# Fused attention and feed-forward on one core: a new load order, a weight product by halves, six banks for value blocks, and zeros in the opening's gaps

## The chip, the cores and the metric

The kernel runs on one core of a Trainium2 chip. The metric is the device time of one execution in microseconds. The comparison uses the median of repeated runs; the profile is of one execution. TensorE multiplies matrices into PSUM (eight banks), ScalarE (ACT) and VectorE (DVE) copy and transform, GpSimd (POOL) and SyncE (SP) here mostly issue DMAs.

## The reference

Inputs are float32: q, k, v of shape (8, 12, 448, 64), two gains of 64, and four weights.

```python
q_n, k_n = rmsnorm(q, g_q), rmsnorm(k, g_k)          # over head_dim = 64
attn = softmax(q_n @ k_n.T / sqrt(64))               # per batch and head, 448 x 448
x = (attn @ v), heads side by side                   # (3584, 768)
a, b = x @ w1, x @ w2                                # (3584, 1024)
out = ((a * b) @ w3) @ w_out                         # (3584, 768)
```

## The kernel before

**Work units.** Attention is cut into 24 units of four heads: three units make one batch of 448 tokens. The norms of q and k are taken on ACT and DVE, q and k are transposed (units 0 to 4 on TensorE, the later ones by DMA), and a unit then has seven score blocks (`do_score`, L626). Each score block is exponentiated by ACT straight out of two PSUM banks (L648). When all seven are done, a value block follows: `do_pv_main` (L711) multiplies the exponentials with ones (for the sums) and with the even and the odd value columns, three kinds in all. Two units are mostly taken together (`start_pv` with size 2); their last 64 rows then go as row-packed matmuls in `do_pv_rest` (L690). A value block of size 2 starts when `PV_BANKS` banks are free, and for as many kinds as there are free pairs of banks the row-packed part goes first; for the others it comes at the end. While a value block is ready and waits for banks, no score and no new pair is started.

**Feed-forward.** w3 and w_out are multiplied with each other first: w3 arrives in eight pieces (`load_w3`), each is transposed on TensorE (`do_w3_turn`, L1071) and copied, and then a "pair" (`w34_pair`) makes 128 rows of the product w3 w_out. A pair holds two PSUM banks and consists of passes of four 64x64 matmuls (L799 in `do_pass`); in the second half of a pair the two row halves swap banks. Between the halves stands `hand_over`: a no-operation on SP (on POOL, once w2 is in) that waits for the first half's last matmul and that the second half waits for. The passes of each half that need the second half of w_out wait for it. Afterwards `ffn1_pair` multiplies x with w1 and w2, and `ffn2_pair` multiplies a*b with the product; those are pairs too. The third buffer for exponentials lies in w_outs, so it comes free when the product is complete.

**Order.** A planner in the kernel lays all instructions out in program order, with costs and due times of its own. TensorE's next step is chosen in `pe_try`: value blocks, transposes, the running pair, scores, a new pair. At most `MAX_PAIRS` pairs are open. A score goes ahead of a running pair only when it is `hungry`, that is when ACT is nearly out of work. The loads that convert weights and v to bfloat16, and q and k of units 1 to 5, are issued by POOL in the order of `POOL_ORDER`:

```python
    POOL_ORDER = (
        "w0 w1 o0 w2 o1 q1 v0 w3 w4 q2 w5 v1 w6 w7 v2 a0 a1 a2 q3 b0 v3 b1 q4 b2 q5".split()
    )
```

Here w is a piece of w3, o a half of w_out, a and b are thirds of w1 and w2, q stands for q and k of a unit, and v for the four loads of a unit's values. A load is issued by POOL only when the one eight before it has landed.

**Start and end.** TensorE starts on matmuls of zeros (`warm`, L1226). The last 128 rows of the output are made by `do_last` (L991) in two parts, each stored by two DMAs (L1005); the other tiles are stored by two DMAs of 64 partitions each from SP (L938).

Of the kernel before, what the change touches and what calls it, by code (L numbers as in the profile page):

```python
# [195 lines left out]
def kernel(  # L196
# [43 lines left out]

    N_PE_T = 5
    QUAD = 13.0
    WARM = 18
    MAX_PAIRS = 2
    MARGIN = 0.25
    LOW = 2
    PV_BANKS = 4
    SOON = 0
    AHEAD_W3 = 4
    EARLY = 4  # L250
    STOCK = 14
    PACE = 1.7
    POOL_ORDER = (
        "w0 w1 o0 w2 o1 q1 v0 w3 w4 q2 w5 v1 w6 w7 v2 a0 a1 a2 q3 b0 v3 b1 q4 b2 q5".split()
    )
    ON_POOL = (1, 2, 3, 4, 5)

# [510 lines left out]
    running = [None]  # L768

    class Pair:  # L770
        def __init__(self, name, nk, n, ready, sides, evacuate):
            self.name, self.nk, self.n = name, nk, n
            self.sides, self.evacuate = sides, evacuate
            self.phase, self.pos, self.gap_at = 0, 0, 0.0
            self.needs = ready

        def ready(self):
            return max(self.gap_at, self.needs(self.pos))

    def hand_over(p, mm, t):  # L780

        at = t + 0.23
        e = "SP" if max(w_at["w2"]) == INF else "POOL"
        nop = (nc.sync if e == "SP" else nc.gpsimd).nop()  # L784
        tc.add_manual_dep(
            nop.ins, mm.ins.name, SYNC_DEP, reason="first half of the sums complete"
        )
        free[e] = max(free[e], at)
        p.gap_at = free[e] + 0.15
        p.nop = nop  # L790

    def do_pass(p, t):
        took = pass_us(p.n) + into("n")
        first = None
        for r in range(2):
            z = r ^ p.phase
            lhsT, rhs = p.sides[z](p.pos)
            for h in range(2):
                mm = nc.tensor.matmul(  # L799
                    out=ps_all[64 * h : 64 * h + 64, p.bank + z, 0 : p.n],  # L800
                    lhsT=lhsT[64 * r : 64 * r + 64, 64 * h : 64 * h + 64],
                    rhs=rhs[64 * r : 64 * r + 64],
                    start=(p.phase == 0 and p.pos == 0),
                    stop=(p.phase == 1 and p.pos == p.nk - 1),
                    tile_position=(64 * r, 64 * h),
                    skip_group_check=True,
                )
                first = first or mm
        if p.phase == 1 and p.pos == 0:
            tc.add_manual_dep(  # L810
                first.ins, p.nop.ins.name, SYNC_DEP,
                reason="the other row half takes over the bank",
            )
        p.pos += 1
        running[0] = p
        if p.pos == p.nk:
            running[0] = None
            p.pos = 0
            p.phase += 1
            if p.phase == 1:  # L820
                hand_over(p, mm, t)
            else:
                pairs.remove(p)
                p.evacuate(p, t + took + TO_ENGINE - 0.187)
        return took

    def start_pair(p, z):
# [10 lines left out]
    def w34_pair(fc):  # L838
        def evacuate(p, at):
            z = p.bank  # L840

            def done(e):
                freed(z)(e)
                w34_at.append(e + SEM)

            add(
                None, {"ACT": 0.70, "DVE": 0.89}, -800.0,
                lambda e: copy_on(
                    e,
                    w34s[:, fc, :].rearrange("p (z n) -> p z n", z=2),  # L850
                    ps_all[:, z : z + 2, 0:NH],
                ),
                needs=[lambda: at], done=done,
            )

        side = lambda nh: lambda gc: (
            w3T[:, gc, fc * 128 : (fc + 1) * 128],
            w_outs[:, gc, nh * NH : (nh + 1) * NH],
        )
        return Pair(  # L860
            "w", CF, NH,
            lambda pos: max(w_at["w3T"][fc], w_at["w_out"][pos // (CF // 2)]) + SEM,
            (side(0), side(1)), evacuate,
        )

    a_sb = {}
# [61 lines left out]
    def ffn2_pair(bp, t):  # L928
        def evacuate(p, at):
            z = p.bank  # L930
            hold = {}

            def copy(engine):
                hold["o"] = out_pool.tile([128, 2, NH], FP, tag="o_sb", name="o_sb")
                copy_on(engine, hold["o"], ps_all[:, z : z + 2, 0:NH])

            def store(x):
                nc.sync.dma_start(  # L938
                    out=out_rows(bp, t, x),
                    in_=hold["o"][HP * x : HP * x + HP].rearrange("p z n -> p (z n)"),  # L940
                )

            def copied(e):
                freed(z)(e)
                for x in range(2):
                    add(
                        "SP", 0.57, -20.0, lambda x=x: store(x),
                        needs=[lambda: e + SEM], moves=(0.55, 0.14),
                    )

            add(
                None, {"ACT": 0.7, "DVE": 0.89}, -500.0, copy,
                needs=[lambda: at], done=copied,
            )
            o_used[bp].append(at)

        def ready(pos):
            return max(all_of(w34_at, CF), tile_at(bp, t)) + SEM

        side = lambda nh: lambda fi: (  # L960
            abT[bp][:, fi, t * 128 : (t + 1) * 128],
            w34s[:, fi, nh * NH : (nh + 1) * NH],
        )
        return Pair("o", CF, NH, ready, (side(0), side(1)), evacuate)

    def out_rows(bp, t, x):
        bb, j = divmod(2 * t + x, NJ)
        r0 = (2 * bp + bb) * S
        return out[r0 : r0 + S].rearrange("(p j) n -> j p n", j=NJ)[j]
# [9 lines left out]
    def do_last(t, z):  # L979


        x = last_x[0]
        last_x[0] += 1
        bp, tl = B // 2 - 1, NT - 1
        c0 = tl * 128 + HP * x
        w = NH // 2
        for fi in range(CF):
            for c in range(2):
                for nh in range(2):
                    n0 = nh * NH + c * w  # L990
                    nc.tensor.matmul(  # L991
                        out=ps_all[HP * nh : HP * nh + HP, z + c, 0:w],
                        lhsT=abT[bp][:, fi, c0 : c0 + HP],
                        rhs=w34s[:, fi, n0 : n0 + w],
                        start=(fi == 0), stop=(fi == CF - 1),
                        tile_position=(0, HP * nh), skip_group_check=True,
                    )
        took = 2 * CF * pass_us(w) + into("l")
        bank_at[z] = bank_at[z + 1] = INF
        o_sb = out_pool.tile([128, 2, NH], FP, tag="o_sb", name="o_sb")  # L1000
        ends = []

        def store(nh):
            eng = nc.scalar if nh and x else nc.sync
            eng.dma_start(  # L1005
                out=out_rows(bp, tl, x)[:, nh * NH : (nh + 1) * NH],
                in_=o_sb[HP * nh : HP * nh + HP, 0],
            )

        def done(e):  # L1010
            ends.append(e + SEM)
            if len(ends) == 2:
                for nh in range(2):
                    add(
                        "ACT" if nh and x else "SP", 0.6, -500.0 + nh,
                        lambda nh=nh: store(nh), needs=[lambda: max(ends)],
                    )

        for c, (e, us) in enumerate((("DVE", 0.27), ("ACT", 0.25))):
            add(  # L1020
                e, us, -500.0,
                lambda e=e, c=c: copy_on(
                    e, o_sb[:, 0, c * w : (c + 1) * w], ps_all[:, z + c, 0:w]
                ),
                needs=[lambda: t + took + TO_ENGINE_WIDE - 0.16], done=done,
            )
        return took
# [59 lines left out]
        return took  # L1087

    def next_pair(t):
        if len(pairs) >= MAX_PAIRS:  # L1090
            return None
        return next((p for p in waiting if p.ready() <= t), None)

# [15 lines left out]
    def pe_step(t):  # L1109

        took = pe_try(t, t - MARGIN)
        return pe_try(t, t) if took is None else took

    def start_pv(t, size, idle):

# [39 lines left out]
    def pe_try(t, r):  # L1155
# [10 lines left out]
            return start_pv(t, 2, idle)  # L1166
        two = adjacent(idle)
        score = score_ready(r) and out_scores[0] < 2 and two is not None and size != 2
        hungry = free["ACT"] <= t + 0.3 and out_scores[0] == 0
        if mode[0] == "t":  # L1170
            took = any_turn(t, r, idle, 1)
            if took is not None:
# [1 line left out]
        if running[0] and running[0].ready() <= r:  # L1174
            if score and hungry:
                return do_score(t, two)
            return do_pass(running[0], t)
        took = any_turn(t, r, idle, 2)
        if took is not None:
            return took  # L1180
        new = next_pair(r)
# [26 lines left out]
    with tc.manual_schedule():  # L1208
# [22 lines left out]
        def g_product():  # L1231
# [13 lines left out]
                lhsT=gp_row.rearrange("a x d -> a (x d)"), rhs=ones_row[:, 0:1],  # L1245
                start=True, stop=True,
            )
            warm(4)

        def spread():  # L1250
            nc.vector.tensor_copy(out=g_b, in_=ps_all[:, 6, 0:D])
            nc.vector.tensor_copy(out=g_col, in_=ps_all[:, 6, D : D + 1])

        warm(WARM)
        free.update(ACT=4.0, DVE=4.0, SP=4.0, POOL=2.3, PE=7.6)
        plan.now = plan.moved_to = 2.2
        plan.moving["SP"].append([2.3, 2.6, lambda t: None, 0.086])
        landed[0].update(q=4.5, k=5.4)
# [65 lines left out]
```

## Time and profile before

| | |
|---|---|
| median of 13 runs | 359.66 us (358.34 to 363.79) |
| the profiled execution | 360.47 us, its span 358.7 us |
| mean granted TensorE clock | 0.993 |
| busy: PE, ACT, DVE, POOL | 347.0, 261.6, 207.7, 75.5 us |
| DMA, moved in all | 55.11 MB, mean 154 GB/s |

The span runs from the first to the last instruction of the profiled execution, and the run's own time lies 1.8 us above it. PE is TensorE's matmul track, PEld its weight loads. SPq, POOLq and ACTq are the sequencers that issue DMAs and wait for semaphores. In a timeline a line has the start, the duration, the engine, the line of the kernel, the operation, what it writes and reads, the tile shape and the count; in brackets stands idle time before it and what ended it. A busy TensorE is not the same as a TensorE at its peak, since the ends of matmuls are modelled.

### The profile page before, as it was taken

The page shows a single profiled execution, that of the slowest core. Times are in us where ns is not written, and L with a number is a line of the kernel's source. Part 1 is how long each engine was busy: PE and PEld are TensorE (multiplying, and loading weights), DVE is VectorE, ACT ScalarE, POOL GpSimd, SP SyncE. Part 2 cuts the span into 40 slices and gives each one's busy share as a digit, 9 for nine tenths or more (in the row PEclk, how much of TensorE's full clock was granted, in tenths as well). Part 3 has the DMA queues.
Part 4 walks back from the last instruction along what each step waited for, and adds up shares of the span by engine and source line. Part 5 has one row for each costly group of instructions (what it writes and reads, how often), then busy time and mean ns, then how long its engine had stood idle before and what let it go on. Part 6 is the DMA issues. An engine that isn't in the chain of part 4 may idle for free.

```text
span 358.7 us, 16164 instructions
## 1 busy us (share of the span) xinstructions
PE 347.0 (97%) x7358; PEld 221.3 (62%) x7358; DVE 207.7 (58%) x293; ACT 261.6 (73%) x375; POOL 75.5 (21%) x132
## 2 busy tenths in 40 slices
PE   8699999999999999999999999999999999999995
PEld 3377756656665666656657566576665657666673
DVE  4258477897999887696578774465363330122200
ACT  4748787998996998988999799778686932222131
POOL 7267351304200505005032040400320000000000
PEclk9989999999999999999999999999999999999999
DMA  8999998759999999966699769942291005200056
GB/s 186 223 273 189 265 263 237 141 125 221 174 215 286 178 197 285 188 109 129 178 227 176 222 86 232 242 76 47 45 191 33 4 2 126 56 4 2 14 131 170
DMA packets 68360, 55.11 MB, mean 154 GB/s; under 512 B 44932, under 2 KB 62244, under 8 KB 68292
## 3 DMA queue, kind: packets, MB, share of 16 engines
q1 hardware_dynamic: 49904, 36.61, 43.8%
q0 software_dynamic: 18016, 16.92, 27.3%
q8 instruction: 57, 0.93, 1.1%
q10 hardware_dynamic: 372, 0.56, 0.5%
q14 instruction: 11, 0.09, 0.1%
HBM read 46.66 MB, written 11.01 MB: 161 GB/s over the span
## 4 chain that ended last, share of the span: by engine, by line
PE 85%; ACT 8%; DMA 4%; issue 1%; POOL 1%; POOLq 0%; ACTq 0%; SPq 0%
PE ps_all L799 60%; PE ps_all L711 12%; PE ps_all L626 8%; DMA w_outs<-in_moe_w_out_dram 4%; ACT P L648 4%; PE ps_all L690 2%; ACT sq L414 1%; ACT Pr L648 1%; PE ps_all L991 1%; PE ps_all L1049 1%; ACT w_outs L648 1%; PE ps_all L1071 1%; ACT a_sb L324 0%; POOL w3s L392 0%; ACT o_sb L324 0%
## 5 line engine op out<-in xcount | busy, mean ns | idle before, releaser
L648 ACT ACTIVATE P<-ps_all 128x896 bf16<-128x896 f32 x120 | 105.1, 918 | 11.9 <-PE ps_all L626 11.8
L363 POOL DMA_DIRECT2D v_sb<-in_v_dram x96 | 57.3, 616 | 174.6 <-PE ps_all L799 120.4
L799 PE MATMUL ps_all<-xT,w2s 64*64 64x448 bf16 x1536 | 89.2, 349 | 0.3 <-ACT P L648 0.3
L799 PE MATMUL ps_all<-xT,w1s 64*64 64x448 bf16 x1536 | 89.3, 349 | 0.0
L799 PE MATMUL ps_all<-w34s,abT 64*64 64x384 bf16 x1728 | 79.3, 323 | 0.4
L882 DVE TENSOR_TENSOR abT<-ps_all,a_sb 128x896 bf16<-128x896 f32 x32 | 34.8, 1088 | 60.1 <-PE ps_all L799 51.5
L799 PEld LDWEIGHTS <-abT 64*64 64x64 bf16 x1728 | 52.2, 107 | 20.5 <-POOLq L784 1.6
L626 PE MATMUL ps_all<-qkT 64*64 64x448 bf16 x672 | 60.8, 352 | 2.8 <-ACT P L648 1.3
L799 PEld LDWEIGHTS <-w2s 64*64 64x64 bf16 x1536 | 47.3, 107 | 25.4 <-issue 1.6
L799 PEld LDWEIGHTS <-w1s 64*64 64x64 bf16 x1536 | 47.0, 107 | 25.3 <-issue 0.4
L421 DVE TENSOR_REDUCE ssq<-sq 128x14 f32<-128x896 f32 (+1 forms) x50 | 51.2, 1041 | 15.8 <-ACT sq L414 15.6
L444 DVE TENSOR_TENSOR qks<-qk_sb,al 128x448 bf16<-128x448 f32 x96 | 55.7, 618 | 4.9 <-ACT al L433 4.6
L414 ACT ACTIVATE sq<-qk_sb 128x896 f32<-128x896 f32 (+1 forms) x50 | 45.0, 917 | 4.0 <-DMA qk_sb<-in_q_dram 3.9
L753 DVE TENSOR_TENSOR xT<-ps_all,r 128x448 bf16<-128x448 f32 x48 | 28.1, 618 | 20.0 <-ACT r L734 19.0
L324 ACT ACTIVATE o_sb<-ps_all 128x768 f32<-128x768 f32 (+1 forms) x22 | 17.0, 771 | 27.8 <-PE ps_all L799 26.2
L324 ACT ACTIVATE a_sb<-ps_all 128x896 bf16<-128x896 f32 x20 | 18.3, 917 | 23.0 <-PE ps_all L799 23.0
L626 PEld LDWEIGHTS <-qkT 64*64 64x64 bf16 x672 | 21.5, 106 | 16.2 <-issue 5.5
L648 ACT ACTIVATE w_outs<-ps_all 128x896 bf16<-128x896 f32 x24 | 21.6, 915 | 8.4 <-PE ps_all L626 8.3
L799 PE MATMUL ps_all<-w_outs,w3T 64*64 64x384 bf16 x512 | 25.8, 340 | 1.3 <-DMA w_outs<-in_moe_w_out_dram 1.2
L711 PE MATMUL ps_all<-P,v_sb 128*32 128x448 bf16 x480 | 26.0, 352 | 0.0
L711 PEld LDWEIGHTS <-v_sb 128*32 128x32 bf16 x592 | 15.9, 97 | 12.1
L648 ACT ACTIVATE Pr<-ps_all 128x896 bf16<-128x896 f32 x24 | 22.1, 919 | 0.1
(60 smaller groups left out, 213.8 us busy)
## 6 DMA issues: line engine op xcount, KB each, us to landing
out_dram<-o_sb SPq DMA_DIRECT2D x54, 192.0 KB, 3.7
qk_sb<-in_q_dram SPq DMA_DIRECT2D x18, 448.0 KB, 4.3
qk_sb<-in_k_dram SPq DMA_DIRECT2D x18, 448.0 KB, 5.0
v_sb<-in_v_dram POOLq DMA_DIRECT2D x48, 64.0 KB, 4.1
v_sb<-in_v_dram POOLq DMA_DIRECT2D x48, 48.0 KB, 4.3
qk_sb<-in_q_dram POOLq DMA_DIRECT2D x5, 448.0 KB, 9.4
qk_sb<-in_k_dram POOLq DMA_DIRECT2D x5, 448.0 KB, 10.2
w3s<-in_moe_w_dram POOLq DMA_DIRECT2D x8, 256.0 KB, 6.2
```

The source lines that it names most:

```text
L324: nc.scalar.activation(out=out, in_=in_, func=AF.Copy, scale=1.0 if by is None else by)
L363: nc.gpsimd.dma_start(out=v_bufs[i % 4][p0 : p0 + HP, g::2, 0 : j1 - j0].rearrange("p h j d -> p h (j d)"), in_=src[:, g::2, j0:j1].rearra ...
L414: nc.scalar.activation(out=s["sq", t][:, x0:x1], in_=src[:, t, x0:x1], func=AF.Square)
L421: nc.vector.tensor_reduce(out=s["ssq"][:, t, x0:x1], in_=s["sq", t][:, x0:x1], axis=AX, op=ADD)
L444: nc.vector.tensor_tensor(out=s["qks"][:, t, :, x], in0=src[:, t, x], in1=s["alpha"][:, t, x].unsqueeze(2).broadcast_to([NP, NJ, D]), op=MULT,
L626: nc.tensor.matmul(out=sc[HP * c : HP * c + HP, u, 0:S].rearrange("p (j s) -> p j s", j=NJ), lhsT=qkT[u * D : (u + 1) * D, 1, j, cols], rh ...
L648: lambda: nc.scalar.activation(out=dst, in_=sc[:, :, 0:S], func=AF.Exp),
L690: nc.tensor.matmul(out=ps_all[hd * HALF : (hd + 1) * HALF, banks[x], 0:S], lhsT=(v_bufs[(i + x) % 4][g : g + HP, hd, NF, kind - 1 :: 2] if ...
L711: nc.tensor.matmul(out=ps_all[hd * HALF : (hd + 1) * HALF, z, 0:S], lhsT=value_weights(i, hd, j, kind), rhs=s["P"][:, hd, j, :] if j < NF ...
L753: lambda: nc.vector.tensor_tensor(out=xT[b][:, 2 * m + kind - 1, :], in0=ps, in1=s["r"], op=MULT),
L799: mm = nc.tensor.matmul(out=ps_all[64 * h : 64 * h + 64, p.bank + z, 0 : p.n], lhsT=lhsT[64 * r : 64 * r + 64, 64 * h : 64 * h + 64], rhs= ...
L882: nc.vector.tensor_tensor(out=abT[bp][:, f0 : f0 + 2, odd * S : (odd + 1) * S], in0=ps_all[:, z : z + 2, 0:S], in1=a_sb[b, f0], op=MULT,)
```

## The change

- `POOL_ORDER` begins with the first half of w_out; some parts of w3, w1 and the values move as well.
- The first three pairs of the product (`SPLIT = 3`) run by halves of w_out: all passes of both row halves that need the first half of w_out come first, then those of the second. A pair then has two hand-overs instead of one. Until the second half of w_out has landed in the plan, three pairs may be open (`EARLY_PAIRS`) and a single piece of w3 is transposed as soon as it is there.
- A double value block starts on six free banks instead of four.
- When fewer than six attention or feed-forward pairs wait (`STARVED`), a score may overtake a running pair while ACT still has 0.9 us of work in the plan (0.3 before). As before, this holds only when no score waits for its exponential (`ONE` is 0).
- In the plan's first 13 us, TensorE gets a matmul of zeros of 256 columns wherever it would have nothing to do and a bank is free. The zeros at the start are 15 instead of 18, and those behind the product of the gains 1 instead of 4.
- Output tiles whose 128 rows lie in one batch are stored by one DMA, except in the last two batches.
- The last 128 rows go out of a q/k buffer that is no longer used, and their stores alternate between SP and ACT in both parts.

```diff
-    WARM = 18
+    WARM = 15
+    WARM_TO = 13.0
+    WARM_N = 256
-    PV_BANKS = 4
+    PV_BANKS = 6
+    STARVED = 6
+    HUNGRY = 0.9
+    ONE = 0
+    SPLIT = 3
+    EARLY_PAIRS = 3
...
-        "w0 w1 o0 w2 o1 q1 v0 w3 w4 q2 w5 v1 w6 w7 v2 a0 a1 a2 q3 b0 v3 b1 q4 b2 q5".split()
+        "o0 w0 w1 w2 o1 q1 v0 w3 w4 q2 a0 v1 w5 w6 v2 w7 a1 v3 q3 b0 a2 b1 q4 q5 b2".split()
...
+            part = nk // halves
+            self.steps = [
+                (x ^ y, part * y + pos)
+                for y in range(halves) for x in range(2) for pos in range(part)
+            ]
...
-            (side(0), side(1)), evacuate,
+            (side(0), side(1)), evacuate, 2 if fc < SPLIT else 1,
...
+            whole = bp < B // 2 - 1 and 2 * t // NJ == (2 * t + 1) // NJ
...
+                if whole:
+                    add(
+                        "SP", 0.6, -20.0, store_whole,
+                        needs=[lambda: e + SEM], moves=(1.1, 0.14),
+                    )
+                    return
...
-        o_sb = out_pool.tile([128, 2, NH], FP, tag="o_sb", name="o_sb")
+        spare = qk_bufs[0].rearrange("p w x j d -> p (w x j d)")
+        o_sb = spare[:, x * NH : (x + 1) * NH].rearrange("p (z n) -> p z n", z=1)
...
-            eng = nc.scalar if nh and x else nc.sync
+            eng = nc.scalar if nh else nc.sync
...
-        if len(pairs) >= MAX_PAIRS:
+        if len(pairs) >= (EARLY_PAIRS if w_at["w_out"][1] == INF else MAX_PAIRS):
...
-        return pe_try(t, t) if took is None else took
+        took = pe_try(t, t) if took is None else took
+        if took is None and t < WARM_TO and idle_banks(t):
+            return do_warm(single(idle_banks(t)))
+        return took
+
+    def do_warm(z):
+
+        nc.tensor.matmul(
+            out=ps_all[:, z, 0:WARM_N], lhsT=warm_t[:, 0:128], rhs=warm_t[:, 0:WARM_N],
+            start=True, stop=True,
+        )
+        into("t")
+        return pass_us(WARM_N)
...
-        hungry = free["ACT"] <= t + 0.3 and out_scores[0] == 0
+        low = sum(p.name != "w" for p in waiting) < STARVED
+        hungry = free["ACT"] <= t + (HUNGRY if low else 0.3) and out_scores[0] <= (
+            ONE if low else 0
+        )
...
-        took = any_turn(t, r, idle, 2)
+        took = any_turn(t, r, idle, 1 if w_at["w_out"][1] == INF else 2)
...
-            warm(4)
+            warm(1)
...
-        free.update(ACT=4.0, DVE=4.0, SP=4.0, POOL=2.3, PE=7.6)
+        free.update(ACT=4.0, DVE=4.0, SP=4.0, POOL=2.3, PE=7.2)
```

More of the change, by code (lines that the diff above doesn't have):

```diff
@@ L770, with __init__, changes @@
     class Pair:
-        def __init__(self, name, nk, n, ready, sides, evacuate):
-            self.name, self.nk, self.n = name, nk, n
+        def __init__(self, name, nk, n, ready, sides, evacuate, halves=1):
+            self.name, self.n = name, n
             self.sides, self.evacuate = sides, evacuate
-            self.phase, self.pos, self.gap_at = 0, 0, 0.0
-            self.needs = ready
-        def ready(self):
-            return max(self.gap_at, self.needs(self.pos))
+            self.k, self.gap_at, self.needs = 0, 0.0, ready
+            part = nk // halves
[3 more added lines that the diff above has]
+            ]
+        def ready(self):
+            return max(self.gap_at, self.needs(self.steps[self.k][1]))
+        def changes(self):
+            return 0 < self.k < len(self.steps) and (
+                self.steps[self.k][0] != self.steps[self.k - 1][0]
+            )
     def hand_over(p, mm, t):
@@ L794, in do_pass @@
         first = None
+        swap, pos = p.steps[p.k]
         for r in range(2):
-            z = r ^ p.phase
-            lhsT, rhs = p.sides[z](p.pos)
+            z = r ^ swap
+            lhsT, rhs = p.sides[z](pos)
             for h in range(2):
@@ L802, in do_pass @@
                     rhs=rhs[64 * r : 64 * r + 64],
-                    start=(p.phase == 0 and p.pos == 0),
-                    stop=(p.phase == 1 and p.pos == p.nk - 1),
+                    start=(p.k == 0), stop=(p.k == len(p.steps) - 1),
                     tile_position=(64 * r, 64 * h),
@@ L808, in do_pass @@
                 first = first or mm
-        if p.phase == 1 and p.pos == 0:
+        if p.changes():
             tc.add_manual_dep(
@@ L813, in do_pass @@
             )
-        p.pos += 1
+        p.k += 1
         running[0] = p
-        if p.pos == p.nk:
+        if p.k == len(p.steps):
             running[0] = None
[L818 to L824, printed above, removed]
+            pairs.remove(p)
+            p.evacuate(p, t + took + TO_ENGINE - 0.187)
+        elif p.changes():
+            running[0] = None
+            hand_over(p, mm, t)
         return took
@@ L935, in copy, with store_whole @@
                 copy_on(engine, hold["o"], ps_all[:, z : z + 2, 0:NH])
+            flat = lambda: hold["o"].rearrange("p z n -> p (z n)")
+            whole = bp < B // 2 - 1 and 2 * t // NJ == (2 * t + 1) // NJ
             def store(x):
                 nc.sync.dma_start(
-                    out=out_rows(bp, t, x),
-                    in_=hold["o"][HP * x : HP * x + HP].rearrange("p z n -> p (z n)"),
-                )
+                    out=out_rows(bp, t, x), in_=flat()[HP * x : HP * x + HP]
+                )
+            def store_whole():
+                bb, j = divmod(2 * t, NJ)
+                r0 = (2 * bp + bb) * S
+                rows = out[r0 : r0 + S].rearrange("(p j) n -> j p n", j=NJ)
+                nc.sync.dma_start(out=rows[j : j + 2], in_=flat())
             def copied(e):
                 freed(z)(e)
+                if whole:
[4 more added lines that the diff above has]
+                    return
                 for x in range(2):
@@ L1014, in done @@
                     add(
-                        "ACT" if nh and x else "SP", 0.6, -500.0 + nh,
+                        "ACT" if nh else "SP", 0.6, -500.0 + nh,
                         lambda nh=nh: store(nh), needs=[lambda: max(ends)],
@@ L1168, in pe_try @@
         score = score_ready(r) and out_scores[0] < 2 and two is not None and size != 2
-        hungry = free["ACT"] <= t + 0.3 and out_scores[0] == 0
+        low = sum(p.name != "w" for p in waiting) < STARVED
+        hungry = free["ACT"] <= t + (HUNGRY if low else 0.3) and out_scores[0] <= (
+            ONE if low else 0
+        )
         if mode[0] == "t":
```

## The prediction

> **What bounds the kernel now.** I read the page's first part, then the chain of waits in order of time, then the windows of the opening, then TensorE's timeline around the value blocks and at the end.
>
> ```profile
> PE 347.0 (97%) x7358; PEld 221.3 (62%) x7358; DVE 207.7 (58%) x293; ACT 261.6 (73%) x375; POOL 75.5 (21%) x132
> PE 85%; ACT 8%; DMA 4%; issue 1%; POOL 1%; POOLq 0%; ACTq 0%; SPq 0%
> ```
>
> TensorE is occupied in 97% of the span and carries 85% of the chain. From 291 us on only feed-forward work is left, 60 us of it back to back. So a microsecond that TensorE gains earlier moves the end by a microsecond, as long as it has work. The question is where TensorE does not do useful work. The largest place is the opening:
>
> ```profile
> 4.74 14.24 DMA w_outs<-in_moe_w_out_dram
> 18.98 0.04 issue
> 19.03 7.07 PE ps_all L799 x128
> ```
>
> The chain waits until 19.0 us for the second half of w_out. Then come 128 matmuls, 32 passes of four, in 7.07 us. In a later stretch of the same chain 44 of them (11 passes) take 1.79 us, 0.163 us each, so 32 should take 5.2. The windows (stretch and its length, busy time of PE, PEld, DVE, ACT and POOL, the granted clock, DMA share, GB/s) show why:
>
> ```profile
> 12.26:15.67 3.41, 2.63 (x52) 1.49 (x53) 0.07 (x1) 2.85 (x4) 0.78 (x2) 1.00 1.14 206
> 15.67:19.08 3.41, 1.55 (x24) 0.90 (x23) 0.53 (x1) 2.93 (x4) 0.39 (x1) 1.00 1.09 328
> 19.08:22.50 3.42, 3.42 (x48) 2.67 (x51) 1.25 (x2) 1.95 (x3) 2.11 (x4) 0.51 1.23 213
> ```
>
> TensorE was busy 1.55 us of 3.41 before 19.08, and then had half its clock for 3.42 us. The DMA share stays above 1: the loads are a second bound of the opening.
>
> **What the Trainium skill says.** "TensorE: Matmul & The Clock Gate", section "What's actually happening": the clock is halved after an idle window of about 3.4 us and comes back after a busy one; the windows run freely. The trace agrees: zeros of 512 columns are 0.43 us apart until 5.4 us, then 0.21, and the slow stretch lasts 3.42 us. What busy share is enough, the page doesn't say; here 2.63 of 3.41 us (77%) kept the clock and 1.55 (45%) lost it. "DMA: Bandwidth & Descriptors", section "Issuing engines are not separate DMA queues": all queues share 16 engines. So a new order of the loads makes none faster in sum; the share of 1.09 to 1.23 agrees. "Perfetto Trace Analysis", section "Identifying the Most-Contended Engine": busy time of matmuls is no measure of headroom. Agreed: 15 score matmuls at 82.67 take 1.38 us, where 15/4 passes of 0.19 make 0.71.
>
> **A. Half of w_out first, product by halves, three pairs open: -1.5 us.** POOL's eight-deep queue dates the landings, because each later issue waits for an older load: first w3 piece 9.0, second 10.3, first w_out half 14.0, third piece 15.4, second half 19.0. A piece is thus 1.2 to 1.4 us, a half 3.8. The same five loads now come as half, three pieces, half. I put the half's end at 9.0 + 2.6 = 11.6 and the pieces at 12.9, 14.1 and 15.4; the second half stays at 19.0. Before 19.03 TensorE did eight passes of the product (32 matmuls at 13.99). Now 24 are permitted, 16 more, at most 16 x 0.163 = 2.6 us. But the first pair can't start before piece one is transposed (0.62) and copied (0.7 to 1.0), about 14.4. From there to 19.0 are 4.6 us, which also hold two transposes of pieces (1.24) and four or five scores (0.19 each, 0.9). That leaves 2.5 us, 15 passes, seven more than before: 1.1 us. With the half microsecond by which the first scores can come sooner (the q and k transposes stand at 10.5 behind a wait for piece two, their input done at 9.97) I take -1.5; ends 0 and -2.6. Each of three pairs has two hand-overs instead of one: a no-operation on SP, which still carries only q/k loads there; it ended one wait of 0.5 us in all. Another pair or a score covers it: 0, at most +1.5.
>
> **B. Zeros in the gaps and a fuller window: -1.9 us.** The fill stops near 13 us, so it is not the zeros but the added passes that must fill 15.7 to 19.1: 1.55 us plus most of 1.1 to 2.6 makes 2.6 or more, the share that kept the clock. Gain 7.07 - 5.2 = 1.9; ends 0 and -1.9. The zeros themselves (256 columns, half of the 0.21 us of 512) lie in gaps before 13 us, where TensorE waited for loads and qkT; one too many delays by 0.11: 0, at most +0.3. The three zeros fewer at the start and three after the g product were followed by a wait of 0.38 us for a load: 0.
>
> **C. Six banks: -0.8 us.** Of eleven double value blocks one had six free banks:
>
> ```profile
> 49.33 0.38 PE L690 MATMUL ps_all<-Pr,ones 64*32 64x448 bf16 x8
> ...
> 53.54 0.84 PE L799 MATMUL ps_all<-w_outs,w3T 64*64 64x384 bf16 x16
> ```
> ```profile
> 76.70 0.38 PE L690 MATMUL ps_all<-Pr,ones 64*32 64x448 bf16 x8
> ...
> 80.72 0.38 PE L690 MATMUL ps_all<-Pr,v_sb 64*32 64x448 bf16 x8
> 81.03 0.95 PE L799 MATMUL ps_all<-xT,w2s 64*64 64x448 bf16 x16
> ```
>
> Both do the same 96 matmuls; the first takes 4.21 us to the next work, the second, with its last eight row-packed ones behind, 4.33. Ten blocks save 0.12 each: -1.2. The added wait: with two pairs open four banks are taken, and the block must let one finish and be emptied, while new pairs and scores are held back. Emptying is 0.81 (ACT) to 1.09 us (DVE) plus some 0.2. The other pair's second half, six passes of 0.19 = 1.13, or eight of 0.163 = 1.3, lies beside it. I charge +0.4 over all ten; ends 0 and +11 (a whole 1.1 each). ScalarE's scores wait too; after 100 us it has slack.
>
> **D. Hungrier scores: -0.7 us.** A score may now overtake a pair while ScalarE has 0.9 us of work left. TensorE idles 0.51 us in 60-100 and 0.82 in 100-150, and loses some 0.6 in the scores at 82.67 because ScalarE holds it up: 1.9 visible. I take a third; ends +0.5 (banks that pairs then miss) and -1.9.
>
> **E. End: -0.2 us.**
>
> ```profile
> 353.83 1.82 SPq L1005 DMA_DIRECT2D out_dram<-o_sb  x3
> 354.91 0.54 ACTq L1005 DMA_DIRECT2D out_dram<-o_sb  x1
> ```
>
> The last copies end at 354.87; SP issues its third store until 355.65, ACT until 355.45. With two on each, SP's last ends with ACT's. The q buffer in place of an output tile removes a wait that the trace does not show at that place: 0. Eighteen of the 27 other output tiles leave as one store: SP saves 18 issues of 0.59 us, but nothing on the chain waits for SP: 0, between -0.3 and +0.3.
>
> **F. The later loads: +0.5 us.** a0 (w1's first third) and v1 now precede w5; v2 precedes w7; a2 comes behind v3, q3 and b0. By POOL's waits q2 and k2 land at 26.3 and 27.6, a0, a1, a2 at 36.7, 39.2, 41.8: 2.5 to 2.7 us each; b0 at 46.6. So w5 moves from 28.6 to about 33, w7 to about 37, a2 to about 48.3. Pairs 5 to 7 started after transposes at 37.1; 3.4 us ahead, TensorE asks near 33.7, just as w5 lands. The first use of w1 was 55.2, now near 51.5, 3 us after a2. I charge +0.5; ends 0 and +2.5. q3 (now behind two thirds of w1, not three, but v3) lands about a microsecond sooner.
>
> **Sum.** -1.5 - 1.9 - 0.8 - 0.7 - 0.2 + 0.5 = -4.6. The profiled execution took 360.47 us, 358.7 of span and 1.8 around it, and would come to 355.9 (span 354.1). The median of the 13 runs is 359.66, 0.8 below it; I take the difference from that: 355.1.
>
> **Rivals.** *The clock drops all the same* (17%). Row transposes or sparse passes may leave the window under the share needed, and its phase is free. For it: the fill ends before the window. Against: 24 passes permitted. -4.6 + 1.9 = -2.7: 357.0. In that case the zeros do nothing, which is also the case of a change that doesn't do what it says.
> *The loads become the bound* (17%). What TensorE gains before 24 us it waits for at w5 to w7 and before a2. For it: DMA share over 1 to 60 us, w5 later by 4. Against: transposes of three pieces waited together until 37. Of A and B's 3.4 some 0.9 stay: -0.9 - 0.8 - 0.7 - 0.2 = -2.6: 357.1.
> *Six banks cost more than they save* (11%), the one that ends slower. Place: ahead of each double block; price: an evacuation that the other pair doesn't cover. At 0.7 us uncovered, +7 - 1.2, and with the rest at -3.8: +2.0, 361.7. It decides from 0.5 us a block: (3.8 + 1.2)/10. For it: DVE works in order and is 86 to 89% busy in 60-150. Against: two open pairs are half a pair apart, and four of six banks are often free already.
>
> **Numbers.** The forecast has 55%, its own range 353 to 357.3. A measurement here tells about 0.3% from no change, 1.1 us. The gains of all parts at their best make 7.8 us, 351.9; the two middle rivals reach to about 359. The range of 351.6 to 359.2 leaves out most of the third rival and the far ends. Faster: nearly all of the forecast and nine tenths of the middle two, 0.84; slower: most of the last, 0.10; the rest 0.06.
>
> **What would show it.** Granted clock 1.0 in 19-23 us and 0.163 us per pass; some 20 passes of the product before the second half lands; first half landed near 11.6; TensorE idle under 1 us between 23 and 50; the first pass through w1s near 51; every double block in 4.2 us, with under 0.2 us idle ahead of it; the end of the last matmul near 350. Idle of TensorE between 26 and 45 ended by w3s or w1s would speak for the loads; idle ahead of L690 for the banks; a time above 359 would refute the sum.

## The result, and the profile after

The changed kernel takes 438.59 us (median of 11 runs, 434.11 to 443.52), against 360.0 for the kernel before: a ratio of 1.2153, 95% interval 1.2121 to 1.2185. The prediction was 355.1. It is wrong in sign and by 83 us.

The first part of the page, and the first line of the chain of waits:

```profile
span 436.0 us, 16154 instructions
PE 369.7 (85%) x7380; PEld 237.3 (54%) x7380; DVE 213.3 (49%) x299; ACT 258.6 (59%) x369; POOL 75.4 (17%) x132
PE 67%; DMA 17%; ACT 6%; issue 4%; SPq 3%; DVE 3%; POOLq 0%; DVEq 0%; ACTq 0%
```

TensorE is 66 us idle where it was 12, and the DMAs hold 17% of the chain where they held 4. The places that the prediction watched look as forecast. The same windows of the opening as in the prediction (stretch, length, busy time of PE, PEld, DVE, ACT and POOL, granted clock, DMA share, GB/s):

```profile
12.26:15.67 3.41, 3.41 (x60) 2.18 (x62) 1.75 (x3) 3.16 (x5) 1.26 (x3) 1.00 1.15 209
15.67:19.08 3.41, 3.26 (x84) 2.45 (x80) 0.32 (x1) 2.50 (x3) 0.55 (x1) 1.00 1.12 333
19.08:22.50 3.42, 3.42 (x92) 3.04 (x88) 1.39 (x2) 2.31 (x4) 2.05 (x4) 1.00 1.24 222
```

TensorE is busy in 3.26 of the 3.41 us after which the kernel before lost its clock, and keeps it; 92 matmuls run after 19.08 where 48 did. A double value block, from TensorE's timeline:

```profile
74.95 0.38 PE L697 MATMUL ps_all<-Pr,ones 64*32 64x448 bf16 x8
75.16 0.56 PE L697 MATMUL ps_all<-Pr,v_sb 64*32 64x448 bf16 x16
75.65 1.32 PE L718 MATMUL ps_all<-P,ones 128*32 128x448 bf16 x24
76.79 2.44 PE L718 MATMUL ps_all<-P,v_sb 128*32 128x448 bf16 x48
79.17 0.38 PE L633 MATMUL ps_all<-qkT 64*64 64x448 bf16 x4
```

From 74.95 to 79.17 are the 4.22 us forecast. Up to 85 us the kernel is ahead: TensorE runs 752 matmuls between 50 and 85 us, where it ran 704. Then the stores of whole output tiles begin (L966). SP's timeline from there:

```profile
85.62 2.20 SPq L966 DMA_DIRECT2D out_dram<-o_sb  x2
89.06 15.87 SPq L518 DMA_TRANSPOSE qkT<-qks  x2
105.03 0.61 SPq L346 DMA_DIRECT2D qk_sb<-in_q_dram  x1
105.73 0.45 SPq L346 DMA_DIRECT2D qk_sb<-in_k_dram  x1
106.27 0.53 SPq L966 DMA_DIRECT2D out_dram<-o_sb  x1
```

Two transposes keep SP for 15.87 us after two such stores. In the kernel before, after four half stores, it was 3.28:

```profile
89.92 2.46 SPq L938 DMA_DIRECT2D out_dram<-o_sb  x4
92.48 3.28 SPq L511 DMA_TRANSPOSE qkT<-qks  x2
```

What TensorE waited for in the changed kernel:

```profile
PE ps_all L633 <- DMA qkT<-qks: 21.0, 4, 11.5
PE ps_all L633 <- ACT r L740: 18.7, 4, 14.0
PE ps_all L718 <- issue: 10.2, 3, 5.1
```

The columns are the sum, the number and the longest. A score can't start before its transposed q and k have landed. The waits on ACT go back to DMAs as well, to the loads of q and k. The longest of them:

```profile
290.23 0.95 ACT L421 ACTIVATE sq<-qk_sb 128x896 f32<-128x896 f32 x1 [13.81 <-DMA qk_sb<-in_k_dram]
291.66 0.53 PE L633 MATMUL ps_all<-qkT 64*64 64x448 bf16 x1 [13.98 <-ACT r L740]
```

By the profile, ACT itself had stood 13.81 us at a load of k; the reciprocal `r`, which frees banks for scores, comes after it in ACT's order. On the chain of waits the loads of q and k hold 9% of the span and the transposes 8%.

Idle time is not the whole loss. TensorE's busy time grew too, from 347.0 to 369.7 us, and its granted clock fell around its long waits:

```profile
265.00:290.00 25.00, 7.54 (x132) 3.46 (x125) 2.55 (x3) 1.87 (x2) 0.00 (x0) 0.66 0.79 92
```

The granted clock is 0.66 on average in these 25 us and 0.918 over the whole execution (0.993 before); a matmul of the w1 passes takes 370 ns on average where it took 349. The loss lies in a part that I had costed at nothing.

### The profile page after: what moved, and what is told of

Read it like the earlier page. It is cut to its first block, busy times and chain, and to the rows that moved or that the text cites. A ratio compares the mean times of both kernels' runs of the same rounds, so it can differ in the third digit from the quotient of the medians.

```text
span 436.0 us, 16154 instructions
## 1 busy us (share of the span) xinstructions
PE 369.7 (85%) x7380; PEld 237.3 (54%) x7380; DVE 213.3 (49%) x299; ACT 258.6 (59%) x369; POOL 75.4 (17%) x132
## 4 chain that ended last, share of the span: by engine, by line
PE 67%; DMA 17%; ACT 6%; issue 4%; SPq 3%; DVE 3%; POOLq 0%; DVEq 0%; ACTq 0%
PE ps_all L819 48%; DMA qkT<-qks 8%; PE ps_all L718 7%; PE ps_all L633 7%; DMA qk_sb<-in_k_dram 5%; DMA qk_sb<-in_q_dram 4%; SPq L518 3%; ACT sq L421 2%; PE ps_all L1273 1%; DVE qks L451 1%; PE ps_all L697 1%; ACT w_outs L655 1%; ACT P L655 1%; PE ps_all L1081 1%; PE ps_all L1103 1%
## 5 line engine op out<-in xcount | busy, mean ns | idle before, releaser
L633 PE MATMUL ps_all<-qkT 64*64 64x448 bf16 x672 | 70.2, 369 | 42.1 <-DMA qkT<-qks 21.0
L819 PE MATMUL ps_all<-xT,w2s 64*64 64x448 bf16 x1536 | 99.3, 372 | 3.4 <-issue 3.4
L819 PE MATMUL ps_all<-xT,w1s 64*64 64x448 bf16 x1536 | 98.8, 370 | 3.2 <-issue 3.2
L819 PE MATMUL ps_all<-w34s,abT 64*64 64x384 bf16 x1728 | 81.8, 323 | 2.2 <-ACT r L740 1.3
L819 PEld LDWEIGHTS <-w2s 64*64 64x64 bf16 x1536 | 54.1, 114 | 32.1 <-issue 10.2
L819 PEld LDWEIGHTS <-w1s 64*64 64x64 bf16 x1536 | 54.6, 113 | 29.2 <-issue 8.1
L819 PEld LDWEIGHTS <-abT 64*64 64x64 bf16 x1728 | 55.2, 107 | 20.2 <-issue 3.5
L633 PEld LDWEIGHTS <-qkT 64*64 64x64 bf16 x672 | 27.7, 109 | 59.1 <-issue 28.2
L718 PE MATMUL ps_all<-P,v_sb 128*32 128x448 bf16 x480 | 30.0, 375 | 10.2 <-issue 10.2
L331 ACT ACTIVATE o_sb<-ps_all 128x768 f32<-128x768 f32 x13 | 10.6, 812 | 22.0 <-PE ps_all L819 22.0
```

The lines of the kernel that those rows point to most:

```text
L331: nc.scalar.activation(out=out, in_=in_, func=AF.Copy, scale=1.0 if by is None else by)
L633: nc.tensor.matmul(out=sc[HP * c : HP * c + HP, u, 0:S].rearrange("p (j s) -> p j s", j=NJ), lhsT=qkT[u * D : (u + 1) * D, 1, j, cols], rh ...
L718: nc.tensor.matmul(out=ps_all[hd * HALF : (hd + 1) * HALF, z, 0:S], lhsT=value_weights(i, hd, j, kind), rhs=s["P"][:, hd, j, :] if j < NF ...
L819: mm = nc.tensor.matmul(out=ps_all[64 * h : 64 * h + 64, p.bank + z, 0 : p.n], lhsT=lhsT[64 * r : 64 * r + 64, 64 * h : 64 * h + 64], rhs= ...
```

## The experiments

**Theories.** S: the whole-tile store is the cause; P: another part is. Within S, E: the store's destination, `rows[j : j + 2]`, begins with a dimension of 2, and so the store runs on two of the sixteen DMA engines. The Trainium skill says so in "DMA: Bandwidth & Descriptors", section "Why a DMA increments its semaphore by 16 and not by 1": for each access pattern the slowest dimension that isn't 1 counts, and the number of engines is the largest up to 16 that divides both. Source 128, destination 2: two engines. Z: one store of 384 KB is too long, whatever its shape.

**e1_two_halves: the one store as two, in the same place of the same program order.**

```diff
-                rows = out[r0 : r0 + S].rearrange("(p j) n -> j p n", j=NJ)
-                nc.sync.dma_start(out=rows[j : j + 2], in_=flat())
+                store(0)
+                store(1)
```

> The changed kernel with its plan and program order kept; only the one store of a whole output tile is issued as two stores of 64 partitions. Theory S (the whole store is the cause, whatever the reason): the waits of 8 to 15 us behind transposes and q/k loads go, and the rest of the change shows what it is worth: 354 to 356 us. Theory P (other parts, such as six banks or the load order, cause the waits, the store only stands beside them): stays above 420 us.

Measured: 357.4 us, ratio to before 0.9927 (0.9899 to 0.9955). Theory S stands, P falls: one form of store in 18 places costs 81 us. The rest of the change is worth 2.8 us, not the 4.6 forecast.

**e2_whole_only: the kernel before with nothing but the whole stores** (`store_whole`, `whole` and the branch in `copied` from the change's diff).

> The kernel before, with nothing but the whole-tile stores (18 of them, 18 half stores left). Theory S: at least 420 us, some 80 us over the kernel before, with SP's transposes lasting 8 to 15 us where they follow a whole store. Theory P: 358 to 361 us.

Measured: 436.23 us, ratio 1.2106 (1.2041 to 1.2171). The store is also enough by itself. SP's timeline of this kernel shows the same picture (another whole store was issued 12 us earlier):

```profile
105.93 0.53 SPq L949 DMA_DIRECT2D out_dram<-o_sb  x1
106.58 11.62 SPq L511 DMA_TRANSPOSE qkT<-qks  x2
```

**e3_rows128 and e4_rows2x64: the same bytes, the same rows, two shapes.**

```diff
# e3_rows128
-                r0 = (2 * bp + bb) * S
-                rows = out[r0 : r0 + S].rearrange("(p j) n -> j p n", j=NJ)
-                nc.sync.dma_start(out=rows[j : j + 2], in_=flat())
+                r0 = (2 * bp + bb) * S + 64 * (j - bb)
+                nc.sync.dma_start(out=out[r0 : r0 + 128], in_=flat())
...
# e4_rows2x64: the same r0, and in place of the last line
+                rows = out[r0 : r0 + 128].rearrange("(p a) n -> a p n", a=2)
+                nc.sync.dma_start(out=rows, in_=flat())
...
```

In both, the half stores of the same batches move to the 64 rows that are left (not shown). The output's rows come out in another order here, as in the next two runs.

> The changed kernel, same plan and order, but the 18 whole stores write 128 neighbouring rows (and the 18 half stores of these batches 64 neighbouring rows): the rows of the output are thus permuted. One store still moves 384 KB from 128 partitions, but the first dimension of its destination is 128 instead of 2. Theory E (a store whose destination begins with a dimension of 2 is spread over two DMA engines, as the Trainium skill, DMA: Bandwidth & Descriptors, states of the slowest dimension): no stall, 354 to 356 us. Theory Z (one store of 384 KB is too long for the queue, whatever its shape): above 420 us.

> As the run with 128 neighbouring rows, the same 18 stores over the same rows, but the destination is written as 2 x 64 rows (every second row), again a permutation of the output. Theory E: the stall is back, 430 to 445 us. Theory Z: as slow as the run with 128 rows. If the place of the rows in memory (neighbours instead of every seventh) were what helps, this one would stay fast too, at about 355 us.

Measured: 357.16 us (ratio 0.9926, 0.9905 to 0.9947) and 440.01 us (1.2267, 1.2183 to 1.235). Z falls, and so does the idea that the place of the rows in memory matters: each store writes the same block of 128 rows in both. e3_rows128's timeline, with two stores of 384 KB ahead of the transposes:

```profile
85.31 2.04 SPq L967 DMA_DIRECT2D out_dram<-o_sb  x2
88.75 3.32 SPq L518 DMA_TRANSPOSE qkT<-qks  x2
```

**e5_rows8x16 and e6_rows4x32: the dose** (`a=8`, `a=4` in e4_rows2x64's line).

> As the runs with 128 neighbouring rows and with 2 x 64 rows, the same 18 stores over the same rows, now written as 8 x 16 rows (the output's rows are permuted again). Theory E, that the first dimension sets the number of DMA engines: eight engines with 16 rows each, 16 x 0.12 = 1.9 us per store in place of 7.7 on two; 357 to 361 us, and 18 x 8 = 144 completion packets in place of 36, so about 67,928 packets on the page. A theory that any destination of two dimensions is slow: above 420 us.

> The same with 4 x 32 rows. Theory E: four engines with 32 rows each, 3.9 us per store; the time lies between the runs with 8 and with 2, 362 to 395 us, and the page has about 67,856 packets. A theory that any destination of two dimensions is slow: above 420 us.

Measured: 364.84 us (1.011, 1.0057 to 1.0164) for eight, 393.71 us (1.093, 1.0869 to 1.0991) for four. The first is 4 us above the range that I expected of it. The profile also counts the engines. Of the page's third part, the packet totals of e1_two_halves, e3_rows128, e5_rows8x16, e6_rows4x32 and the changed kernel, in this order:

```profile
DMA packets 68360, 55.12 MB, mean 155 GB/s; under 512 B 44932, under 2 KB 62244, under 8 KB 68292
```
```profile
DMA packets 68071, 55.10 MB, mean 156 GB/s; under 512 B 44644, under 2 KB 61956, under 8 KB 68004
```
```profile
DMA packets 67927, 55.10 MB, mean 152 GB/s; under 512 B 44500, under 2 KB 61812, under 8 KB 67860
```
```profile
DMA packets 67855, 55.10 MB, mean 141 GB/s; under 512 B 44428, under 2 KB 61740, under 8 KB 67788
```
```profile
DMA packets 67819, 55.10 MB, mean 126 GB/s; under 512 B 44392, under 2 KB 61704, under 8 KB 67752
```

By the same section of the skill each engine that takes part ends with one increment of the semaphore. Thirty-six half stores on sixteen engines end with 576 of them, 18 whole stores on k engines with 18 k. So the totals should be 68360 - 576 + 18 k: 68072, 67928, 67856 and 67820 for sixteen, eight, four and two. Each is met but for one packet. The records of 4-byte packets alone, 4739 in e1_two_halves and 4451, 4307, 4235 and 4199 in the others, meet the same differences exactly.

| first dimension | engines | rows per engine | engine time of one store | median us |
|---|---|---|---|---|
| 128 | 16 | 8 | 1.0 us | 357.16 |
| 8 | 8 | 16 | 1.9 us | 364.84 |
| 4 | 4 | 32 | 3.9 us | 393.71 |
| 2 | 2 | 64 | 7.7 us | 440.01 |

The engine time is an estimate: the rows per engine by 0.121 us, the median time of a 3072-byte packet (one row) in the changed kernel's records. The loss against 128 rows is 0.4, 2.0 and 4.6 us per store, so between four and seven tenths of the added engine time reaches the end. The records also show the two engines at their limit: from 277 to 289 us of the changed kernel 17 packets of stored rows start in every microsecond, and 17 by 0.121 us are 2.06 engines' time. With four engines the most is 34 a microsecond, in the first pair of stores.

**e7_whole_on_act: the changed kernel's store, issued by ScalarE's queue** (`nc.scalar` in place of `nc.sync`; the planner counts the 18 issues on ACT, so the order of the program is laid out anew).

> The changed kernel's own whole store (destination 2 x 64 rows, right rows), but issued by ScalarE's queue instead of SP's. Theory R (transposes and loads are slow because they stand behind the store in the same queue of two DMA engines): with a queue of its own the store takes turns with them, so most of the stall goes: below 385 us. Theory B (the two engines are simply full, whoever issues): above 410 us. ScalarE pays 18 issues of about 0.55 us.

Measured: 427.17 us, ratio 1.1828 (1.1757 to 1.1899). Theory R falls. SP no longer issues the stores, and its pairs of transposes still last 8 and 13 us:

```profile
89.19 8.16 SPq L518 DMA_TRANSPOSE qkT<-qks  x2
97.44 0.58 SPq L346 DMA_DIRECT2D qk_sb<-in_q_dram  x1
98.11 4.37 SPq L346 DMA_DIRECT2D qk_sb<-in_k_dram  x1
102.66 12.96 SPq L518 DMA_TRANSPOSE qkT<-qks  x2
```

A queue of its own saves 11 of 81 us. That agrees with the section that the prediction quoted, that all queues share the engines: the two engines' time is used up, whoever issues. How transposes and loads wait on these two engines is argued; the records don't say which engine a packet ran on.

**e8_halves_four_banks: e1_two_halves with `PV_BANKS = 4`.**

> The changed kernel with two half stores for each tile (the run e1_two_halves), and value blocks starting on four free banks again. By the prediction's step C six banks are worth 0.8 us: this run 0.5 to 1.2 us above e1_two_halves, double value blocks of 4.33 instead of 4.21 us. Rival: the wait for six banks costs what it saves, both alike within 0.3 us.

Measured: 361.56 us, ratio 1.0049 (1.0029 to 1.007), 4.2 us above e1_two_halves. One place where TensorE stands still, a double value block that stops halfway and the pair after it:

```profile
131.30 0.56 PE L718 MATMUL ps_all<-P,v_sb 128*32 128x448 bf16 x6 [0.47 <-issue]
131.79 0.38 PE L697 MATMUL ps_all<-Pr,v_sb 64*32 64x448 bf16 x8
132.10 0.36 PE L819 MATMUL ps_all<-w34s,abT 64*64 64x384 bf16 x4
133.37 1.01 PE L819 MATMUL ps_all<-w34s,abT 64*64 64x384 bf16 x20 [0.73 <-ACT o_sb L331]
```

Its last matmul ends near 355.4, e1_two_halves' near 350.3. Of these 5.1 us some 2.3 are idle time (from the windows) and at most 1.2 the ten or so blocks at 0.12; the rest lies inside times that count as busy.

**e11_before_six_banks: the kernel before with `PV_BANKS = 6` alone.**

> The kernel before with nothing but six banks for value blocks. Step C of the prediction, 10 blocks of 0.12 less some waiting: 0.8 us faster, 358.8 to 359.4. If the 4.2 us between e8_halves_four_banks and e1_two_halves is what six banks are worth in any plan: 355.5 to 356.5. Rival: the wait for six banks costs more than it saves here, above 360.5.

Measured: 359.63 us, ratio 1.0012 (0.9989 to 1.0035). No difference by the medians, between the forecast and its rival. The clock blurs this one: 10 of its 22 runs have a mean granted clock under 0.995, of the kernel before beside it 5 of 38, and among the others the medians are 358.4 and 359.0, 0.6 apart where 0.8 was forecast. In any case the 4.2 us of e8_halves_four_banks aren't what six banks are worth in any plan; they are what four cost in that one. The planner lays out the whole program anew for each setting, and I don't hold a cause for the size of either number to be settled.

**e9_halves_old_opening: e1_two_halves with the opening of before.**

```diff
-    SPLIT = 3
-    EARLY_PAIRS = 3
+    SPLIT = 0
+    EARLY_PAIRS = 2
# and POOL_ORDER, WARM, warm(4), PE=7.6 and any_turn's 2 as before; WARM_TO = 0.0
```

> The run e1_two_halves with the whole opening as before: old load order, the product not by halves, two open pairs, transposes of w3 in twos, no zeros in gaps, 18 and 4 zeros at the start. Six banks, the hungrier scores and the end stay. The prediction's steps A and B are worth 3.4 us in a run whose clock drops: 359.5 to 361 us. But of 30 runs of the kernel before, 18 had a mean granted clock of 0.998 or more, that is no drop, so step B should hold in a minority of runs only: 1.5 to 2.5 us above e1_two_halves, 359 to 360.

Measured: 359.42 us, ratio 1.0006 (0.9978 to 1.0035); e1_two_halves had 0.9927. By the ratios, which compare each with the kernel before on its own chip, the opening is worth 0.8%, 2.8 us: without it the whole gain is gone. Without six banks (e8_halves_four_banks) it is gone too, so the parts don't add up.

**e10_halves_no_zeros: e1_two_halves with `WARM_TO = 0.0`.**

> The run e1_two_halves without the zeros in the gaps of the opening (the shorter start stays). By the prediction the zeros themselves are worth 0, since the added passes fill the window that decides: within 0.5 us of e1_two_halves (357.4), and granted clocks of 0.995 and more. Rival: without them the clock drops in the opening, mean clock about 0.993 and 358.5 to 360 us.

Measured: 356.23 us, ratio 0.9919 (0.9884 to 0.9953), alike within the intervals. Two windows of its profiled run:

```profile
15.67:19.08 3.41, 3.26 (x80) 2.62 (x76) 0.00 (x0) 1.74 (x3) 0.55 (x1) 1.00 1.11 334
19.08:22.50 3.42, 3.42 (x91) 2.89 (x80) 2.15 (x3) 2.72 (x5) 2.26 (x4) 1.00 1.21 223
```

In this run the clock stays whole without the zeros: the product's added passes fill the window. But three of the nine runs have a mean granted clock of 0.987 to 0.992, under the 0.995 that I expected, and take 357.7 to 359.3 us; the other six take 354.7 to 356.4. With the new opening and its zeros (e1_two_halves, e3_rows128, e8_halves_four_banks) one run of 51 is under 0.995. So the zeros may well keep the clock in runs that would lose it. Nine runs are few, and the runs at a lower clock have no profile that shows where it dropped. This version and e1_two_halves beat both kernels.

## Why the prediction was wrong

**The step that failed is in part E:** "Eighteen of the 27 other output tiles leave as one store: SP saves 18 issues of 0.59 us, but nothing on the chain waits for SP: 0, between -0.3 and +0.3." It counted what issues the store and not what carries it. The runs put this part at +81 us (changed kernel against e1_two_halves) and +76 us (e2_whole_only against the kernel before). The second half of the sentence was wrong too: SP's loads of q and k feed the transposes, these feed the scores, and scores feed everything. They weren't on the chain only because they landed in time. The cover was named nowhere, and nothing asked what it costs when it goes.

Both facts were in reach. The diff shows a destination of 2 x 64 x 768, and the page quoted for the shared engines states the rule in the section on the semaphore. With it: 64 rows per engine instead of 4 in each half store, an estimated 7.7 us at the packet time, 18 times 7.7 = 139 us of two engines that the transposes and loads need as well. None of the three rivals was about stores, so the range couldn't hold the time.

**Opening, parts A, B and F: right in the order of the landings and in the sum, -2.8 where -2.9 stood** (-1.5 - 1.9 + 0.5). POOL's queue in e1_two_halves dates the first half of w_out at 10.06 (forecast 11.6) and the pieces at 11.3, 12.6 and 13.8, each some 1.5 us ahead of the forecast; the first pass through w1s is at 50.07 (near 51), the last matmul ends near 350 (near 350). The split between A and B is not right: the profiled execution had lost its clock, but of the 30 runs of the kernel before beside e1_two_halves 18 had a mean granted clock of 0.998 or more. So -1.9 is an upper end that holds in a minority of runs, A must be worth more than 1.5, and the near agreement of the sums is partly luck. Among the runs at 0.995 or more, e1_two_halves is 2.7 us below the kernel before and e9_halves_old_opening 0.3: some 2.4 us of the opening have nothing to do with the clock. That zeros do nothing is not shown: the medians are alike without them, but more runs lose clock (e10_halves_no_zeros).

**Part C: -0.8 forecast; no clear difference in the old plan, -4.2 in the new.** The blocks do take 4.22 us instead of 4.33. What stands between this and the end is the order of everything else, which the sum left as it was. The rival that six banks cost more, at its price, falls in both plans. **Part D** wasn't tried by itself. In e9_halves_old_opening D, six banks and the new end together give nothing. **The end** gave nothing that can be told: from the last matmul to the end of the span are 5 us in e1_two_halves and 4 in e3_rows128, with the same stores there.

## What to carry to other kernels

Cost a DMA by the engines that carry it before you cost its issue: read the first dimension of both sides that isn't 1, divide the rows by the engines, multiply by the packet time. Merging two transfers into one saves an issue, but not if the merged destination begins with a short dimension; here even the good form, 128 rows, gave no more than two halves (357.16 and 357.4 us). The profile's packet count shows how many engines took part. And where a part is costed at nothing because "nothing waits for it", name the transfer that has to land in time behind it.

## What the runs showed of the hardware

- One store in 18 places, on two engines instead of sixteen, cost 81 us, although the DMA engines together moved the same 55.1 MB; another issuing queue brought back 11.
- The transposing DMAs were held up: their 256-byte packets had at most 1.7 us in e1_two_halves and up to 13.7 in the changed kernel. The loads of q and k were held up as well, with 9% of the chain.
- Around its long waits TensorE had a lower granted clock, 0.66 on average between 265 and 290 us, and its busy time was 369.7 us against 347.0.
- Whether the clock drops in the opening differs between runs. The kernel before and e11_before_six_banks have the same opening; between 19.08 and 22.50 us the first had 0.51 in its profile, the second 1.00. A single profile can show the rarer case.
